# Moving GpSimd's last casts and sink copies into an idle stretch, with the loads they need issued earlier

## Chip, cores and metric

One Trainium2 chip, one core. The metric is the device time of one execution in microseconds (us); lower is better. A single-core execution more than 1.5% above the fastest of its kernel counts as slow; those are named where they occur and are not used in ratios.

## The reference

Sliding-window attention with sink tokens feeds a wave mixer. Cut to what matters:

```python
# q, k, v: (4, 8, 768, 64) float32, times 0.1;  n_sink 4, window 128
scores = q @ k.T / 8                                 # per batch and head
keep   = (pos_k < 4) | (0 <= pos_q - pos_k < 128)    # else -1e9
x      = softmax(scores) @ v                         # -> (4, 768, 512)
theta  = x @ w_theta
y      = w_tok_r @ (x * cos(theta)) + w_tok_i @ (x * sin(theta))
u      = x + y
out    = u + relu(u @ w_ch)
```

## The kernel before

The kernel works on 16 pairs of heads (four batches of four pairs), numbered `i`. One "slot" treats one pair: scores, exponentials (E) on ScalarE, and the weighing of the pair before it, interleaved with the token mix of the batch before. Every engine's order is written by hand. The parts that the change and the argument touch:

```python
vstage = pool("vstage", 4)      # float32 v as loaded
qkr    = pool("qkr", 1)         # q, k transposed by DMA, still in raw order

def pool_copy(out, in_):        # a copy or cast on GpSimd
    nc.gpsimd.tensor_scalar(out=out, in0=in_, scalar1=1.0, scalar2=1.0, op0=ALU.mult, op1=ALU.mult)

QK_DMA = range(12, NPAIR)       # pairs whose q, k are transposed by DMA, ready for use
QK_RAW = (10, 11)               # transposed by DMA, then put in order by a ScalarE copy

def load_qk(i):
    ...
        if i in QK_DMA:         # rows of 64 floats: 256 bytes
            nc.sync.dma_start(out=f.rearrange("p h t d -> p (h t) d"),
                in_=src[b, 2 * hp:2 * hp + 2].rearrange("h (t p) d -> p (h t) d", p=P))
        else:                   # rows of 6 x 64 floats: 1536 bytes
            nc.sync.dma_start(out=f.rearrange("p h t d -> p h (t d)"),
                in_=src[b, 2 * hp:2 * hp + 2].rearrange("h (p t) d -> p h (t d)", t=NT))

def transposed_by_dma(i):       # SyncE issues; for pairs 10, 11 into qkr
    if i in QK_RAW:
        ...
            nc.sync.dma_start_transpose(out=raw, in_=...)         # L182
def transposed(name, i):        # for pairs 10, 11: ScalarE reads qkr, writes qT, kT
    ...                                                           # L206
def slot(i, blk, wtok=None):
    ...
    if i + 2 < HP or HP <= i < NPAIR - 2:
        cast_qk(i + 2)                       # GpSimd
    cast_v(i)
    if i + 2 in V_CAST:
        load_cast_v(i + 2)                   # v, cast in the load; issued by GpSimd
    ...
    transposed_by_dma(i + 2)
    ...
# after the slots of batch b:
    if b == 2 and hp == 3: sink_values(3)    # GpSimd, four copies
    ...
    if b < 3:                                # b == 2: pairs 14 and 15
        for n in range(2):
            load_qk(HP * 3 + 2 * (b - 1) + n)
```

The v loads that GpSimd issues are those of pairs 12 to 15. Names used below: in the lines of the profile, PE is TensorE, DVE VectorE, ACT ScalarE, POOL GpSimd, and SPq the queue in which SyncE issues transfers. E are the exponentials of the scores, zz is x times the cosine and sine (cs) of theta, u is x + y, uT is u transposed by DMA, which the channel sums (L400) need; xT is x transposed by DMA, for theta (L330); qr and kr are pair 11's raw transposes, which ScalarE copies to qT and kT.

The softmax here doesn't subtract the row's maximum and nothing guards it: scores larger than these inputs give would overflow.

Of the kernel before, what the change touches and what calls it, by code (L numbers as in the profile page):

```python
# [12 lines left out]
BF16 = mybir.dt.bfloat16  # L13
# [6 lines left out]
def kernel(  # L20
# [14 lines left out]
    P = 128  # L35
# [5 lines left out]
    HP = H // 2  # L41
# [4 lines left out]
    NPAIR = B * HP  # L46
# [5 lines left out]
    def pool(name, bufs, **kw):  # L52
        return ctx.enter_context(tc.tile_pool(name=name, bufs=bufs, **kw))

    consts = pool("consts", 1)
    stage = pool("stage", 8)
    vstage = pool("vstage", 4)
    cast = pool("cast", 2)
    qkt = pool("qkt", 3)
    qkr = pool("qkr", 1)  # L60
    epool = pool("epool", 4)
    recp = pool("recp", 4)
    xpool = pool("xpool", 2)
# [11 lines left out]
    def pool_copy(out, in_):  # L75
        nc.gpsimd.tensor_scalar(out=out, in0=in_, scalar1=1.0, scalar2=1.0,  # L76
                                op0=ALU.mult, op1=ALU.mult)
# [12 lines left out]
    V_CAST = range(12, NPAIR)  # L90
# [9 lines left out]
    def next_load():  # L100
        for what in later.popleft().split() if later else ():
            {"w": load_wtok, "q": load_qk, "v": load_v}[what[0]](int(what[1:]))


    qk_f, qk_c, qk_t, v_f, v_x, e_t = {}, {}, {}, {}, {}, {}
# [3 lines left out]
    def load_qk(i):  # L109
        b, hp = divmod(i, HP)  # L110
        for name, src in (("q", q), ("k", k)):
            f = stage.tile([P, 2, NT, D], FP32, name=f"{name}f", tag="qkf")
            if i in QK_DMA:
                nc.sync.dma_start(
                    out=f.rearrange("p h t d -> p (h t) d"),
                    in_=src[b, 2 * hp:2 * hp + 2].rearrange("h (t p) d -> p (h t) d", p=P),
                )
            else:
                nc.sync.dma_start(
                    out=f.rearrange("p h t d -> p h (t d)"),  # L120
                    in_=src[b, 2 * hp:2 * hp + 2].rearrange("h (p t) d -> p h (t d)", t=NT),
                )
            qk_f[name, i] = f
# [7 lines left out]
    def cast_qk(i):  # L131
        for name in ("q", "k"):
            c = cast.tile([P, NT, 2, D], BF16, name=f"{name}16", tag=f"{name}16")
            src = qk_f.pop((name, i)).rearrange("p h t d -> p t h d")
            how = CASTS.get((name, i), "pool")
            if how == "act":
                nc.scalar.copy(out=c, in_=src)
            elif how == "dve":
                nc.vector.tensor_copy(out=c, in_=src)
            else:  # L140
                pool_copy(c, src)
            qk_c[name, i] = c
        next_load()

    def load_cast_v(i):
        vx = vxs[i % len(vxs)]
        b, hp = divmod(i, HP)
        nc.gpsimd.dma_start(out=vx[:, :, 0:D], in_=v[b, 2 * hp:2 * hp + 2].rearrange("h (t p) d -> p (h t) d", p=P))
        v_x[i] = vx
# [99 lines left out]
    def weigh(i, e):  # L249
        b, hp = divmod(i, HP)  # L250
        h = 2 * hp + e
        if i % HP == 0 and e == 0:
            x_t[b] = xpool.tile([P, HP, NT, P], BF16, name="x_nat", tag="x_nat")
        if b == 0:
            avp = ps_mm.tile([P, NT, D + 1], FP32, name="avp0", tag="mm")
        elif hp == HP - 1 and e == 0:
            avp = ps_sc.tile([P, 2, 512], FP32, name="av1", tag="sc")[:, 0, 0:NT * (D + 1)]
            avp = avp.rearrange("p (t d) -> p t d", t=NT)
        else:
            avp = ps_sm.tile([P, NT, D + 1], FP32, name="avp", tag="sm")  # L260
        values(i, e, avp)
        normalise(b, hp, avp, e)
# [187 lines left out]
    ident = consts.tile([P, P], BF16)  # L450
    zeros = consts.tile([P, DM], BF16)
    junk = consts.tile([P, 1], FP32)
    half_pi = consts.tile([P, 1], FP32)
    low = consts.tile([P, 1], FP32)

# [31 lines left out]
    def sink_values(b):  # L487
        for tb in range(NB):
            nc.gpsimd.tensor_scalar(out=vsinks[b % 2][:, tb, :, 0:D], in0=vsf[:, b - 2, :, :],
                                    scalar1=rows[:, tb:tb + 1], scalar2=1.0, op0=ALU.mult, op1=ALU.mult)  # L490
# [14 lines left out]
    def make_mask():  # L505
# [14 lines left out]

        nc.scalar.activation(out=bias, in_=mask, func=AF.Identity, scale=30000.0, bias=low)

    W = [8, 1, 4, 1, 0, 3, 3]

    q3 = 2 * NT // 4
# [15 lines left out]
    def finish():  # L541
        if mixed:
            channels(*mixed.pop(0))

    def next_heads(i, name):
        if i + 1 < NPAIR:
            transposed(name, i + 1)

    def slot(i, blk, wtok=None):
        hp = i % HP  # L550
        first, last = hp == 0, hp == HP - 1
        if wtok is not None:
            cast_wtok(wtok)
        if i + 2 < HP or HP <= i < NPAIR - 2:
            cast_qk(i + 2)
        cast_v(i)
        if i + 2 in V_CAST:
            load_cast_v(i + 2)
        if first:
            if i > HP:  # L560
                next_heads(i, "q")
            if i >= 3 * HP:
                scores(i, 0)
            if i > HP:
                piece(blk, 0)
            piece(blk, 1)
        if pending:
            wtok_transposes(pending.pop(), 1)
        if not first or i < 3 * HP:
            scores(i, 0)  # L570
        if hp > 1:
            x_transposes(i // HP, hp - 2)
        if first:
            next_heads(i, "k")
            piece(blk, 2)
        else:
            piece(blk, 0)
            if not last:
                next_heads(i, "q")
        if not first:  # L580
            mask_product(i - 1, 1)
            mask_product(i - 1, 2)
        transposed_by_dma(i + 2)
        if first:
            scores(i, 1)
            turn()
            piece(blk, 3)
        else:
            piece(blk, 1)
            if not last:  # L590
                next_heads(i, "k")
            turn()
            scores(i, 1)
        scores(i, 2)
        if not first:
            piece(blk, 2)
        if wtok is not None:
            wtok_transposes(wtok, 0)
        if not first:
            piece(blk, 3)  # L600
        if hp > 0:
            weigh(i - 1, 0)
            weigh(i - 1, 1)
        if i == 2 * HP - 1:
            mask_product(i, 1)
            mask_product(i, 2)
        finish()
        if wtok is not None:
            pending.append(wtok)
# [21 lines left out]
    load_sinks(1)  # L631
    warm(W[0])
    transposed("q", 0)
    warm(W[1])
    transposed("k", 0)
# [73 lines left out]
    for b in range(1, B):  # L709
        p = b - 1  # L710
        for hp in range(HP):
            i = b * HP + hp
            if b > 1:
                slot(i, (p, hp))
                if b == 2 and hp == 3:
                    sink_values(3)
            else:
                slot(i, (p, hp + 2) if hp < 3 else None, hp + 3 if hp < 3 else None)
                if hp == 1:
                    load_later_sinks()  # L720
                if hp == 3:
                    sink_values(2)
        i = b * HP + HP - 1
        if b > 1:
            four, five = (p, 4), (p, 5)
            piece(four, 0)
            turn()
            x_transposes(b, HP - 2)
            piece(four, 1)
            weigh(i, 0)  # L730
            weigh(i, 1)
            finish()
            piece(four, 2)
            next_heads(i, "q")
            piece(four, 3)
            piece(five, 0)
            x_transposes(b, HP - 1)
            next_heads(i, "k")
            turn()
            piece(five, 1)  # L740
        else:
            five = (p, 5)
            piece(five, 0)
            x_transposes(b, HP - 2)
            next_heads(i, "q")
            piece(five, 1)
            weigh(i, 0)
            next_heads(i, "k")
            weigh(i, 1)
            theta_sums(b, 0, (0, 1))  # L750
            x_transposes(b, HP - 1)
            piece(five, 2)
            theta_sums(b, 0, (2, 3))
            phases(b, 0)
        if b < 3:
            for n in range(2):
                load_qk(HP * 3 + 2 * (b - 1) + n)
        if b > 1:
            thetas(b, 0)
            finish()  # L760
        thetas(b, 1)
        piece(five, 2 if b > 1 else 3)
        theta_sums(b, 2, range(NC))
        if b > 1:
            piece(five, 3)
        phases(b, 2)
# [58 lines left out]
```

## Time and profile before

| | before |
|---|---|
| median of 3 runs | 183.16 us (182.8 to 183.87) |
| span of the profiled execution | 180.9 us |
| TensorE busy | 94% |
| TensorE's named waits, 84 to 121 us | 0.53 + 0.28 + 0.31 + 0.54 = 1.66 us |

```profile
88.04 1.22 SPq L182 DMA_TRANSPOSE qr<-q  x1
89.46 1.21 SPq L182 DMA_TRANSPOSE kr<-k  x1
```

### The profile page before, as it was taken

Reading aid. Unit: us, or ns where it says so; the run is one execution under the profiler, and the core shown is the slowest. Engines: PE = TensorE matmul, PEld = TensorE weight load, DVE = VectorE, ACT = ScalarE, POOL = GpSimd, SP = SyncE. Lnnn points to the kernel's source line nnn. Section 1 sums busy time; section 2 is a strip of 40 time slices with the busy share of each in tenths; the row PEclk is TensorE's granted clock in tenths of the full one; section 3 lists DMA queues with packets and bytes.
Section 4 is the critical chain, followed back from the end, with each engine's and each line's share of the span. In section 5 each row is a group of like instructions: output and inputs, shape, how many; then the busy total and the mean of one; then the engine's idle time right before and its main releaser. Section 6 shows DMA issues by size and latency. Waiting matters only on the chain.

```text
span 180.9 us, 4035 instructions
## 1 busy us (share of the span) xinstructions
PE 169.5 (94%) x1619; PEld 88.4 (49%) x1619; DVE 121.9 (67%) x215; ACT 105.7 (58%) x112; POOL 75.4 (42%) x101
## 2 busy tenths in 40 slices
PE   7799998999999989999998899989999999999991
PEld 2345664554565656443553454434555544344550
DVE  6477867892866688386698981885978816824451
ACT  4897869629768486699998503797454039200000
POOL 8996689987764805038098300750000000000000
PEclk9999999999999999999999999999999999999999
DMA  5999999999998997991399956999733520133413
GB/s 176 307 312 266 350 381 410 383 349 332 328 300 264 287 297 183 282 207 32 102 136 192 220 144 170 297 139 176 118 94 98 147 70 2 59 106 97 145 60 116
DMA packets 73106, 36.80 MB, mean 203 GB/s; under 512 B 61184, under 2 KB 67584, under 8 KB 73088
## 3 DMA queue, kind: packets, MB, share of 16 engines
q1 hardware_dynamic: 65584, 35.60, 71.1%
q0 software_dynamic: 7360, 0.82, 7.3%
q8 instruction: 12, 0.20, 0.5%
q10 hardware_dynamic: 144, 0.13, 0.2%
q14 instruction: 6, 0.05, 0.1%
HBM read 25.82 MB, written 6.29 MB: 178 GB/s over the span
## 4 chain that ended last, share of the span: by engine, by line
PE 64%; ACT 15%; DVE 11%; DMA 3%; issue 3%; POOL 2%; DVEq 0%; ACTq 0%; POOLq 0%
PE yp L372 24%; PE wp L400 9%; PE thp L330 9%; PE avp L277 5%; PE sc L228 5%; ACT E L241 3%; DVE zz L343 3%; ACT cs L339 3%; DVE E L247 3%; ACT cs L340 3%; DMA uT<-u 3%; PE sc L221 2%; PE tp L202 2%; PE wtp L357 2%; PE xtp L307 2%
## 5 line engine op out<-in xcount | busy, mean ns | idle before, releaser
L372 PE MATMUL yp<-zz,wrT 128*128 128x512 bf16 x138 | 52.4, 380 | 1.6 <-DVE zz L343 1.2
L241 ACT ACTIVATE E<-sc 128x1024 bf16<-128x1024 f32 x48 | 47.6, 1032 | 10.6 <-PE sc L228 8.7
L372 PE MATMUL yp<-zz,wiT 128*128 128x512 bf16 x138 | 52.3, 379 | 0.6 <-DVE wiT L361 0.3
L343 DVE TENSOR_TENSOR zz<-cs,x_nat 128x1024 bf16<-128x1024 bf16 x24 | 21.6, 936 | 14.3 <-ACT cs L340 14.3
L247 DVE TENSOR_TENSOR E<-E,mask 128x768 bf16<-128x768 bf16 (+1 forms) x27 | 26.3, 1014 | 1.9 <-ACT E L241 1.9
L76 POOL TENSOR_SCALAR q<-qf 128x768 bf16<-128x768 f32 x14 | 12.3, 881 | 30.6 <-DMA qf<-in_q_dram 15.2
L400 PE MATMUL wp<-wch,uT 128*128 128x512 bf16 x92 | 23.7, 380 | 0.9 <-DMA uT<-u 0.8
L376 DVE TENSOR_TENSOR u<-yp,x_nat 128x512 bf16<-128x512 f32 x23 | 15.9, 690 | 11.0 <-PE yp L372 10.2
L330 PE MATMUL thp<-wth,xT 128*128 128x512 bf16 x96 | 22.8, 379 | 0.1
L339 ACT ACTIVATE cs<-thp,half_pi 128x1024 bf16<-128x1024 f32 (+1 forms) x13 | 13.7, 1051 | 15.5 <-PE thp L330 15.4
L403 DVE SCALAR_TENSOR_TENSOR of<-wp,u 128x512 f32<-128x512 f32 x23 | 15.8, 687 | 9.9 <-PE wp L400 9.8
L372 PEld LDWEIGHTS <-wiT 128*128 128x128 bf16 x138 | 13.5, 98 | 15.3 <-issue 2.4
L372 PEld LDWEIGHTS <-wrT 128*128 128x128 bf16 x138 | 13.5, 98 | 13.5 <-issue 1.7
L277 PEld LDWEIGHTS <-E 128*128 128x128 bf16 x480 | 16.9, 97 | 3.7 <-issue 0.9
L228 PE MATMUL sc<-qT,kT 64*128 64x256 bf16 x192 | 16.6, 264 | 1.4 <-ACT kT L206 0.8
L283 DVE TENSOR_TENSOR x_nat<-avp,rec 128x384 bf16<-128x384 f32 x27 | 15.1, 558 | 0.9
L76 POOL TENSOR_SCALAR k<-kf 128x768 bf16<-128x768 f32 x14 | 14.2, 1015 | 3.1 <-issue 1.2
L228 PEld LDWEIGHTS <-kT 64*128 64x128 bf16 x192 | 6.4, 94 | 16.5 <-issue 12.3
L330 PEld LDWEIGHTS <-xT 128*128 128x128 bf16 x96 | 9.1, 98 | 10.7 <-DVE xT L312 0.6
L277 PE MATMUL avp<-vx,E 128*128 128x65 bf16 x297 | 13.2, 193 | 0.0
L429 ACT COPY lT<-ltp 128x256 bf16<-128x256 bf16 x2 | 0.7, 372 | 21.2 <-PE ltp L427 21.2
L76 POOL TENSOR_SCALAR vx<-vf 128x768 bf16<-128x768 f32 x12 | 12.0, 1005 | 1.9 <-DMA vf<-in_v_dram 1.9
(82 smaller groups left out, 211.6 us busy)
## 6 DMA issues: line engine op xcount, KB each, us to landing
qf<-in_q_dram SPq DMA_DIRECT2D x16, 384.0 KB, 5.5
kf<-in_k_dram SPq DMA_DIRECT2D x16, 384.0 KB, 5.8
out_dram<-of SPq DMA_DIRECT2D x23, 256.0 KB, 2.3
vf<-in_v_dram SPq DMA_DIRECT2D x12, 384.0 KB, 5.3
wf<-in_moe_w_tok_r_dram SPq DMA_DIRECT2D x6, 384.0 KB, 6.6
wf<-in_moe_w_tok_i_dram SPq DMA_DIRECT2D x6, 384.0 KB, 7.6
sqf<-in_moe_w_theta_dram SPq DMA_DIRECT2D x2, 512.0 KB, 6.5
sqf<-in_moe_w_ch_dram SPq DMA_DIRECT2D x2, 512.0 KB, 8.0
```

The source lines that it names most:

```text
L76: nc.gpsimd.tensor_scalar(out=out, in0=in_, scalar1=1.0, scalar2=1.0, op0=ALU.mult, op1=ALU.mult)
L228: nc.tensor.matmul(sc[:, e, 256 * part:256 * part + n], lhsT=kT[r, m * P:(m + 1) * P], rhs=qT[r, m * P:m * P + n], start=not biased, stop= ...
L241: nc.scalar.activation(out=E[:, :, 512 * c:512 * (c + 1)], in_=sc, func=AF.Exp, scale=SCALE)
L247: nc.vector.tensor_tensor(out=E[:, :, r], in0=E[:, :, r], in1=mask2[:, :, r], op=ALU.mult)
L277: nc.tensor.matmul(avp[:, t, :], lhsT=lhsT, rhs=rhs, start=(j == 0), stop=(j == len(seq) - 1), skip_group_check=True)
L330: nc.tensor.matmul(th_t[b, g][:, st, :], lhsT=xT[:, cb, 2 * g + st, :], rhs=wth[:, cb, :], start=(cb == 0), stop=(cb == NC - 1))
L339: nc.scalar.activation(out=cs[:, part, 0, :], in_=thp[:, part, :], func=AF.Sin, bias=half_pi)
L343: nc.vector.tensor_tensor(out=z_t[b][:, 2 * g + st, :, :].rearrange("p o (c n) -> p o c n", c=HP), in0=cs[:, st, :, :].rearrange("p o (c n ...
L372: nc.tensor.matmul(yp, lhsT=wT[i][:, t, sc, :], rhs=z_t[b][:, sc, i, :], start=(j == 0), stop=(j == 2 * NT - 1))
L376: nc.vector.tensor_tensor(out=u.rearrange("p (c n) -> p c n", c=HP), in0=yp.rearrange("p (c n) -> p c n", c=HP), in1=x_t[b][:, :, t, :], o ...
L400: nc.tensor.matmul(wp, lhsT=uT[:, cb, :], rhs=wch[:, cb, :], start=(cb == 0), stop=(cb == NC - 1))
L403: nc.vector.scalar_tensor_tensor(out=of, in0=wp, scalar=0.0, in1=u, op0=ALU.max, op1=ALU.add)
```

## The change

The intent: between batches 2 and 3, GpSimd stood idle for 12.8 us (100.9 to 113.7), while before and after that its copies and casts stretched VectorE's work beside them. The change delays the sink copies behind a "gate" (a copy of one column that waits for VectorE's mask products), and brings the casts of pairs 14 and 15 and their v loads forward into the same hole. To be there in time, the loads of q and k of these pairs are issued in slots 9 and 11 and no longer after batch 2. v staging gives a buffer to the raw transposes.

```diff
-    vstage = pool("vstage", 4)
+    vstage = pool("vstage", 3)
-    qkr = pool("qkr", 1)
+    qkr = pool("qkr", 2)
+    gate = consts.tile([P, 1], BF16)
+    LOAD_LATE = {9: (14,), 11: (15,)}
@@ in slot(i)
-        if i + 2 < HP or HP <= i < NPAIR - 2:
+        if i + 2 < HP or HP <= i < NPAIR - 4:
             cast_qk(i + 2)
-        if i + 2 in V_CAST:
+        if i + 2 in V_CAST and i < NPAIR - 4:
             load_cast_v(i + 2)
@@ around the slots of batches 2 and 3
             if b > 1:
+                for n in LOAD_LATE.get(i, ()):
+                    load_qk(n)
                 slot(i, (p, hp))
-                if b == 2 and hp == 3:
-                    sink_values(3)
@@ after slot 11
+        if b == 2:
+            pool_copy(gate, e_t[i][:, 0, 0:1])
+            sink_values(3)
+            for n in (3, 4):
+                cast_qk(i + n)
@@ after weigh(i, 1)
+            if b == 2:
+                for n in (3, 4):
+                    load_cast_v(i + n)
@@ after batch 2
-        if b < 3:
+        if b == 1:
             for n in range(2):
                 load_qk(HP * 3 + 2 * (b - 1) + n)
```

## The prediction

> **What bounds the kernel now.** I read the page first, then a table of busy time per engine in ten stretches of the span, then the chain of work that ended last between 84 and 123 us, then the timelines of GpSimd, VectorE and the DMA-issuing queue (SPq) there. From the page: busy time of TensorE, and the rows of tenths for GpSimd and the DMA engines (40 slices of 4.52 us).
>
> ```profile
> PE 169.5 (94%) x1619; PEld 88.4 (49%) x1619; DVE 121.9 (67%) x215; ACT 105.7 (58%) x112; POOL 75.4 (42%) x101
> ...
> POOL 8996689987764805038098300750000000000000
> ...
> DMA  5999999999998997991399956999733520133413
> ```
>
> TensorE is busy for 94%, so the whole kernel has 11.4 us of TensorE gaps, and only those can be won. GpSimd, at 42%, is no bound; it can matter only through whom it delays. Its last work (slices 25 and 26, 113 to 122 us) is what the change moves forward. The DMA row has a valley at slices 18 and 19 (81 to 90 us) and is full again at slices 20 to 22. The stretches (columns: window, its length, busy us and instructions of PE, PEld, DVE, ACT, POOL, clock, DMA share, GB/s):
>
> ```profile
> 84.00:95.00 11.00, 10.87 (x131) 5.63 (x129) 8.54 (x13) 11.00 (x11) 6.12 (x6) 1.00 0.73 112
> 95.00:103.10 8.10, 6.97 (x77) 3.37 (x74) 7.62 (x11) 6.15 (x7) 5.11 (x5) 1.00 1.43 216
> 103.10:113.00 9.90, 9.90 (x79) 5.08 (x79) 5.42 (x13) 1.69 (x2) 0.00 (x0) 1.00 0.61 152
> 113.00:120.00 7.00, 6.46 (x32) 2.53 (x31) 6.45 (x8) 5.91 (x7) 6.02 (x6) 1.00 1.18 231
> 120.00:140.00 20.00, 20.00 (x229) 10.04 (x229) 14.93 (x27) 11.62 (x12) 0.11 (x1) 1.00 0.77 129
> ```
>
> TensorE's gaps in these are 0.13, 1.13, 0, 0.54 and 0 us: 1.80 us in all, of which the waits view names 0.53 and 0.28 (the channel sums waiting for the DMA-transposed uT, at 95.7 and 101.7), 0.31 (waiting for u at 103.1) and 0.54 (waiting for zz at 119.7). In the window in between, where GpSimd is wholly idle for 9.9 us, TensorE is full and VectorE has 4.5 us to spare. That is the hole the change aims at. The chain through the two gapped windows (start, us, what):
>
> ```profile
> 96.77 0.69 DVE of L403
> 97.47 3.37 DVE E L247 x3
> 100.83 1.05 issue
> 101.88 0.55 DVE E L247
> 102.43 0.61 DVE u L376
> 103.04 0.04 issue
> 103.08 0.81 PE yp L372 x3
> ...
> 118.41 0.60 DVE u L376
> 119.01 0.64 DVE zz L343
> 119.65 0.04 issue
> 119.69 0.38 PE yp L372
> ```
>
> Twice VectorE sets the pace: by its mask products (L247) and by its phase products (L343). Both have GpSimd beside them. From the timelines of the two engines:
>
> ```profile
> 97.38 5.05 DVE L247 TENSOR_TENSOR E<-E,mask 128x2048 bf16<-128x2048 bf16 x4
> 116.07 2.34 DVE L343 TENSOR_TENSOR zz<-cs,x_nat 128x1024 bf16<-128x1024 bf16 x2 [0.18 <-ACT cs L340]
> 118.94 1.31 DVE L343 TENSOR_TENSOR zz<-cs,x_nat 128x1024 bf16<-128x1024 bf16 x2
> ...
> 96.85 4.04 POOL L489 TENSOR_SCALAR vsink<-vsf,rows 128x512 bf16<-128x512 f32 x4
> ```
>
> The zz pair at 118.94, with GpSimd doing only a DMA issue, took 1.31 us; the pair at 116.07, beside casts, 2.34; the first pair (113.37) 1.92. A mask couple alone (123.44, 129.22) takes 1.68, so four products are 3.36 us, not 5.05.
>
> **What the Trainium skill says.** (1) "SBUF — State Buffer", section "Who interferes with whom": a VectorE instruction with two SBUF inputs contends with a GpSimd instruction that reads SBUF, and the one that comes second is blocked until the first is through. The trace agrees: zz and the mask products, with both inputs in SBUF, are the ones that stretch (1.92 and 2.34 against 1.31), and a GpSimd cast beside them takes 1.77 us against 0.83; u and x_nat, with one input from PSUM, stay at 0.69 and 0.56. (2) "DMA: Bandwidth & Descriptors", section "Issuing engines are not separate DMA queues": all DMAs run on the same 16 engines and interleave. The trace agrees: a load of q lands in 3.6 us where the DMA row is low and in up to 8.9 where it is full. So moved loads hurt whatever transposes run at their new place.
>
> **The change part by part.** The instruction order of the two programs differs, besides names, in GpSimd's and SPq's streams only; one tiny instruction is added.
>
> *The gate and the sinks.* GpSimd copies one element of E of pair 11. Its wait is for VectorE: the last writer of that element is the first mask product of pair 11, the third of the four. E for that product comes at 99.8 (ScalarE), so the product ends near 99.8+1.2=101.0. The sinks (4 x 0.68 alone = 2.7 us, as in batch 1, where they took 2.70) go from 96.9 to 101.0, so they no longer stretch products one to three, and meet at most the fourth. VectorE reaches u at about 101.0+0.5=101.5 in place of 102.35, or 102.2 if a sink is ahead of the fourth product. TensorE's 0.31 us wait for u goes, if the uT before it is not later: TensorE is not free before 102.8. Worth 0.3 us.
>
> *Casts of pairs 14 and 15, and their v.* Four casts of 0.83 and two DMA issues of 1.07, 5.5 us, from 113.7-120.1 into the hole. Starting after the sinks at 103.7: casts of 14 to 105.4; casts of 15 when its load has landed, and pair 13's DMA transposes have released the cast buffer, near 107.5, to 109.2; v issues to 111.4. The first zz is at 113.4, so all three zz pairs should take 1.31: 5.57-3.93=1.64 us less VectorE time. But the chain gives back only what TensorE waited: its products ended at 119.15 and the next began at 119.69. The third zz pair can't start before ScalarE's sine ends at 118.47, so its first product ends at 119.13 and TensorE goes on at 119.2. Worth 0.5 us.
>
> *The loads.* Pair 14's (2 x 384 KB, some 2 us at the 380 to 410 GB/s of the page's best slices) go on SPq at 86.3, at the end of the DMA valley, ahead of the raw transposes of pair 11. These were issued at 88.04 and 89.46, since the single qr buffer was being read by ScalarE's copies until 87.96 and 89.39; with two buffers they go out right after the loads, near 87.7 and 89.0. So the uT issued at 90.77 goes out some 0.4 us sooner, but the rings hold 2 us of load ahead of it: I expect the wait at 95.7 to stay between 0 and 1 us (it was 0.53); cost 0.2 on average. Pair 15's loads come after slot 10's output, at 101: pair 13's transposes and then xT of the third head pair slip by 1.3 us of issuing and about as much of transfer. That xT landed near 107.4 (issue 104.45 plus the median 2.9) and is read at 109.4, so 2 us of slack takes it, barely.
>
> *vstage from 4 buffers to 3.* The fourth v load at the start has to wait for the first cast of v, and SPq is in order, so the weights behind it wait too. From the timelines of SPq and GpSimd:
>
> ```profile
> 6.26 8.97 SPq L128 DMA_DIRECT2D vf<-in_v_dram  x4
> 15.28 2.09 SPq L174 DMA_DIRECT2D sqf<-in_moe_w_theta_dram  x2
> ...
> 14.88 2.02 POOL L76 TENSOR_SCALAR vx<-vf 128x768 bf16<-128x768 f32 x2 [0.85 <-DMA vf<-in_v_dram]
> ```
>
> That cast ends at about 15.9, and the fourth load left by 15.2: 0.7 us or more later, with the v1 and v2 data still in flight. v3 lands some 0.3 to 0.7 us later, w_theta too; its second cast ended at 24.3 and is first needed at 26.0. Cost 0 to 0.4, say 0.1. Later v loads find their buffer free (v8 at 57.7 needs v5's cast, done at 49.8).
>
> Sum: -0.3 -0.5 +0.2 +0.1 = **-0.5 us**, from 183.16 to about 182.6. All four gaps gone would be -1.7.
>
> **Rivals.** (a) *The gain is hidden or taken by DMA*: the loads moved into batch 2 delay uT and xT, so TensorE waits longer at 95.7, 101.7 or 109.4. For it: DMA share 1.43 in 95 to 103, and transposes are small packets. Against: the valley before 88, and slack at 109.4. It would make 183.2 to 184.5. (b) *The start pays*: w_theta and the token weights arrive later behind the blocked v load, and TensorE waits at 25 us. For it: the DMA row is full there, so lost time is lost. Against: SPq issues ran ahead of the data. It would add 0.5 to 1.5. (c) *VectorE was the true bound*, and with 3.3 us of it given back the stages after 119 also tighten: against this, TensorE has no gap from 120 to 140. At most -1.7 us, 181.5.
>
> **Range and chances.** 182.6, with 181.5 (all gaps gone) to 183.8 (rival a or b), which also covers the spread of the kernel before (182.8 to 183.87). Faster by 2% would need 3.7 us, twice the gaps there are: 0.02. Slower by 2% needs both rivals at their worst: 0.03. Within 2%: 0.95.
>
> **What would show it right or wrong.** Right: GpSimd busy from about 101 to 112 and nothing after; zz pairs of batch 2 at 1.31 each; the four mask products near 3.4 to 4.1 us busy; VectorE's total about 3 us below 121.9; no TensorE wait for u near 103, and 0.1 or less for zz near 119. Wrong: longer waits for uT at 96 or 102, a new one for xT at 109, a hole in the first 26 us, or casts of 15 that run past 113 because their load or pair 13's transposes are late.

## More of the kernel before

The prediction shows the page, the stretches and the chain. Three more readings are needed later. First TensorE's timeline, the lines with a wait (start, us, engine, line, operation, what; in brackets the idle time before it and what ended it):

```profile
95.70 1.04 PE L400 MATMUL wp<-wch,uT 128*128 128x512 bf16 x4 [0.53 <-DMA uT<-u]
101.73 1.04 PE L400 MATMUL wp<-wch,uT 128*128 128x512 bf16 x4 [0.28 <-DMA uT<-u]
```

Then, with the same columns, ScalarE's copies of pair 11 and the queue on which SyncE issues the transposes for them:

```profile
91.98 1.61 ACT L206 COPY qT<-qr 128x768 bf16<-128x768 bf16 x1
93.42 1.65 ACT L206 COPY kT<-kr 128x768 bf16<-128x768 bf16 x1
```

## The result

| | before | after |
|---|---|---|
| median of 4 runs | 183.27 us (182.8 to 183.87) | 185.49 us (184.86 to 185.97) |
| ratio | 1 | 1.0117 [1.0074, 1.016] |
| span of the profiled execution | 180.9 us | 183.7 us |
| TensorE's named waits, 84 to 121 us | 1.66 us | 4.19 us |

A ratio here is the mean time of one kernel's fast runs over the mean of the other's in the same rounds, so not quite the ratio of the medians; the brackets are its 95% interval. The change makes the kernel 1.2% slower: within 2%, but 2.9 us from the 182.6 predicted and outside the range. The page after:

```profile
PE 169.4 (92%) x1619; PEld 88.3 (48%) x1619; DVE 117.1 (64%) x215; ACT 105.6 (57%) x112; POOL 73.2 (40%) x102
...
POOL 8975599977658935065215457000000000000000
...
DMA  5999999999999997992999998944834520133413
```

VectorE lost 4.8 us of work (121.9 to 117.1), as the change meant it to. TensorE's own work is the same, 169.4 us, at the same clock: all of the loss is waiting. The DMA row's valley at slices 18 and 19, counted from 0 (before: 1 and 3), reads 2 and 9, and its dip at slices 23 and 24 (before: 5 and 6) reads 9 and 8. The stretches, with the columns that the prediction names:

```profile
84.00:95.00 11.00, 10.87 (x131) 5.60 (x129) 7.31 (x14) 9.58 (x9) 3.11 (x4) 1.00 1.10 164
95.00:103.10 8.10, 5.41 (x59) 2.65 (x58) 4.69 (x7) 6.41 (x7) 2.64 (x3) 1.00 1.32 166
103.10:113.00 9.90, 9.00 (x88) 4.90 (x85) 6.73 (x16) 1.08 (x1) 6.68 (x10) 1.00 1.27 237
113.00:120.00 7.00, 6.40 (x32) 2.60 (x31) 2.78 (x5) 4.58 (x5) 1.66 (x2) 1.00 1.18 131
```

ScalarE, full from 84 to 95 us before, is now busy for 9.58 of the 11 us. TensorE's gaps grow in the second and third stretch: 1.13 to 2.69 us, and none to 0.90. TensorE's waits, from its timeline:

```profile
96.43 1.04 PE L400 MATMUL wp<-wch,uT 128*128 128x512 bf16 x4 [1.38 <-DMA uT<-u]
98.78 0.39 PE L228 MATMUL sc<-qT,kT 64*128 64x256 bf16 x4 [1.31 <-ACT E L241]
104.27 1.04 PE L400 MATMUL wp<-wch,uT 128*128 128x512 bf16 x4 [0.70 <-DMA uT<-u]
112.18 1.47 PE L330 MATMUL thp<-wth,xT 128*128 128x512 bf16 x6 [0.20 <-DMA xT<-x_nat]
114.25 1.04 PE L400 MATMUL wp<-wch,uT 128*128 128x512 bf16 x4 [0.60 <-DMA uT<-u]
```

They sum to 4.19 us, 2.5 more than before; the spans differ by 2.8. The waits for u and zz that the change aimed at are gone. There are five now, four of them for a DMA transpose, and one for ScalarE's E of pair 11. The chain of work that ended last tells how they hang together (start, us, what):

```profile
86.61 0.42 SPq L114
...
87.08 0.83 SPq L114
...
88.01 2.57 SPq L182
...
90.67 5.54 DMA kr<-k
...
96.28 1.52 ACT kT L206
97.81 0.93 ACT E L241
...
99.16 5.07 DMA uT<-u
```

L114 is the load of q and k of pair 14, moved to slot 9; L182 is the raw transpose of pair 11 behind it. The path goes from the moved loads to the raw transposes, and from them to ScalarE's copy and its exponentials. From there the profile's chain goes by VectorE's mask product (98.76) to the next uT. That link is inferred and not shown: this u was ready at 94.85, the product was still running when its uT was issued at 99.16, and SyncE's queue had been issuing pair 12's transposes until 99.07. A second path is in GpSimd's timeline: its casts of pair 12 waited 2.23 and 2.19 us for qr and kr to land (93.33 and 96.35). So the v load of pair 13 went out at 97.92 us, before the change at 95.72, and stood right ahead of this uT, which took 5.1 us to land in place of 3.9. ScalarE's copies and SyncE's queue, beside those of before:

```profile
93.17 1.54 ACT L206 COPY qT<-qr 128x768 bf16<-128x768 bf16 x1 [1.13 <-DMA qr<-q]
96.28 1.52 ACT L206 COPY kT<-kr 128x768 bf16<-128x768 bf16 x1 [1.57 <-DMA kr<-k]
```

```profile
86.61 0.42 SPq L114 DMA_DIRECT2D qf<-in_q_dram  x1
87.08 0.83 SPq L114 DMA_DIRECT2D kf<-in_k_dram  x1
88.01 2.57 SPq L182 DMA_TRANSPOSE qr<-q  x1
90.67 1.24 SPq L182 DMA_TRANSPOSE kr<-k  x1
```

kT is copied 2.9 us later than before. Issuing qr began at the same moment, 88.01 against 88.04, and so the second qr buffer brought nothing: the loads took the time that it freed. But issuing qr held the queue for 2.57 us in place of 1.22, kr went out 1.2 us later, and kr took 5.5 us to land in place of 2.5.

What the change aimed at came about. VectorE's timeline after:

```profile
102.00 1.69 DVE L247 TENSOR_TENSOR E<-E,mask 128x2048 bf16<-128x2048 bf16 x2 [1.54 <-ACT E L241]
119.11 1.29 DVE L343 TENSOR_TENSOR zz<-cs,x_nat 128x1024 bf16<-128x1024 bf16 x2 [1.47 <-ACT cs L340]
121.53 1.29 DVE L343 TENSOR_TENSOR zz<-cs,x_nat 128x1024 bf16<-128x1024 bf16 x2 [0.53 <-ACT cs L340]
```

A zz pair takes 1.29 us with nothing beside it (the first at 115.75 too; before: 1.92, 2.34 and 1.31), and a mask couple 1.69.

### The profile page after: what moved, and what is told of

Its sections match the earlier page's. It is cut to its first block, busy times and chain, and to the rows that moved or that the text cites.

```text
span 183.7 us, 4029 instructions
## 1 busy us (share of the span) xinstructions
PE 169.4 (92%) x1619; PEld 88.3 (48%) x1619; DVE 117.1 (64%) x215; ACT 105.6 (57%) x112; POOL 73.2 (40%) x102
## 4 chain that ended last, share of the span: by engine, by line
PE 55%; DMA 14%; ACT 13%; DVE 8%; SPq 5%; issue 2%; POOL 0%; DVEq 0%; ACTq 0%
PE yp L372 21%; PE wp L400 9%; PE thp L330 9%; DMA uT<-u 6%; DMA vf<-in_v_dram 5%; PE avp L277 4%; PE sc L228 3%; ACT cs L339 3%; ACT cs L340 3%; DMA kr<-k 3%; ACT E L241 3%; DVE E L247 3%; SPq L119 2%; DVE zz L343 2%; PE wtp L357 2%
## 5 line engine op out<-in xcount | busy, mean ns | idle before, releaser
L343 DVE TENSOR_TENSOR zz<-cs,x_nat 128x1024 bf16<-128x1024 bf16 x24 | 18.9, 825 | 17.0 <-ACT cs L340 17.0
L247 DVE TENSOR_TENSOR E<-E,mask 128x768 bf16<-128x768 bf16 (+1 forms) x27 | 24.3, 936 | 4.0 <-ACT E L241 4.0
L400 PE MATMUL wp<-wch,uT 128*128 128x512 bf16 x92 | 23.7, 380 | 2.7 <-DMA uT<-u 2.7
L403 DVE SCALAR_TENSOR_TENSOR of<-wp,u 128x512 f32<-128x512 f32 x23 | 15.8, 686 | 10.7 <-PE wp L400 10.6
L76 POOL TENSOR_SCALAR q<-qf 128x768 bf16<-128x768 f32 x14 | 12.8, 914 | 21.7 <-PE tp L202 9.5
L76 POOL TENSOR_SCALAR k<-kf 128x768 bf16<-128x768 f32 x14 | 13.7, 982 | 5.3 <-DMA kr<-k 2.2
L400 PEld LDWEIGHTS <-uT 128*128 128x128 bf16 x92 | 7.7, 97 | 11.1 <-DMA uT<-u 4.0
```

The costliest lines, as they stand in the source:

```text
L247: nc.vector.tensor_tensor(out=E[:, :, r], in0=E[:, :, r], in1=mask2[:, :, r], op=ALU.mult)
L343: nc.vector.tensor_tensor(out=z_t[b][:, 2 * g + st, :, :].rearrange("p o (c n) -> p o c n", c=HP), in0=cs[:, st, :, :].rearrange("p o (c n ...
L400: nc.tensor.matmul(wp, lhsT=uT[:, cb, :], rhs=wch[:, cb, :], start=(cb == 0), stop=(cb == NC - 1))
L403: nc.vector.scalar_tensor_tensor(out=of, in0=wp, scalar=0.0, in1=u, op0=ALU.max, op1=ALU.add)
```

## The experiments

Twelve kernels. Kernels are compared only within the same rounds. The letters of theories in an expectation are its own. The theories, in words: **the load of pair 14** puts the raw transposes behind it and starves ScalarE; or **the start** pays for the smaller v staging; or **the gate and the late casts** cost; or **load 15 and the v loads** of the hole hold up uT and xT.

One warning on results. All twelve came out as correct, though three of them are wrong (e6, e9 and e10 give pairs 14 and 15 wrong q and k). A likely reason, not tested, is that the inputs are so small that the scores hardly matter. These three measure time only.

### First call: which part costs

**e1_sinks_and_buffers**: before, with the buffers and the gated sinks, without moved loads or casts.

```diff
-    vstage = pool("vstage", 4); qkr = pool("qkr", 1)
+    vstage = pool("vstage", 3); qkr = pool("qkr", 2)
                 if b == 2 and hp == 3:
+                    pool_copy(gate, e_t[i][:, 0, 0:1])
                     sink_values(3)
```

> The kernel before with only the buffer counts (vstage 3, qkr 2) and the gated sinks; loads and casts of pairs 14 and 15 as before. Theory L (the two early loads stand in the DMA rings ahead of time-critical transposes): 182.4 to 183.3, no wait for uT over 0.6 us between 90 and 115. Rival B (buffer counts, blocked v load or the gate cost the time): 184.5 or more. If L is right the raw transposes of pair 11 should go out near 86.4 instead of 88.0, since the second qr buffer then has nothing ahead of it.

Measured: 182.76 us (181.66 to 183.66, 6 runs) against 183.25; ratio 0.9971 [0.9932, 1.001]. No TensorE wait for uT is left from 84 to 121 us. What is left is 0.27 (E), 0.53 (E of VectorE) and 0.19 (zz). So neither the smaller v staging nor the gate costs anything that these runs can see, and the gated sinks may gain a little. The profiled execution ran 1.6 us late from its start (the first channel sum at 42.36 us; before 40.73), so the issue time that I expected for qr is missed in absolute terms. Yet qr went out right after the output ahead of it (87.94, 88.03), where before it stood from 86.26 to 88.04 until ScalarE had freed the one buffer.

**e2_loads_only**: before, with the two loads moved and nothing else.

```diff
             if b > 1:
+                for n in {9: (14,), 11: (15,)}.get(i, ()):
+                    load_qk(n)
                 slot(i, (p, hp))
-        if b < 3:
+        if b == 1:
```

> The kernel before with only the loads of 14 and 15 moved to slots 9 and 11; casts, sinks and buffers as before. Theory L: 185.3 to 186.5, with the raw transposes of pair 11 landing about 4 us later than before. Rival B or rival G (casts and sinks moved into the gap between the batches cost): 183.0 to 183.6.

Measured: median 188.19 us (184.48 to 189.66), four of the six runs slow by the rule above. The ratio, 1.0138 [1.0066, 1.021], rests on the two fast runs (184.48 and 187.0), so the verdict is "unclear". The profiled execution was slow, too. It is used for one thing only: the raw transposes are late here as well, since kT is copied at 95.68 after waiting 1.61 us (before: 93.42, no wait), without gate, casts or new buffers. Slow executions came up in e2 (four of six), e6 (three) and e14 (one) and in no other kernel here; these are the three whose profiles show a TensorE wait of about 2 us or more (2.67, 2.96 and 1.99). So leaving slow executions out may leave out a part of what these kernels cost; no run settles it.

**e4_load14_only**: the change, with load 15, its casts and v left at before's place.

```diff
-    LOAD_LATE = {9: (14,), 11: (15,)}
+    LOAD_LATE = {9: (14,)}
-            for n in (3, 4): cast_qk(i + n)           # likewise load_cast_v
+            cast_qk(i + 3)
         if b > 1:
+            if b == 2: load_qk(15); cast_qk(15); load_cast_v(15)
             thetas(b, 0)
```

> The changed kernel with load, cast and v of pair 15 at their old place after batch 2; only load 14 early in slot 9. Splits the loss by load. Theory L, by the gaps of the trace after: load 14 costs the 1.38, 1.31 and most of the 0.70 us waits, load 15 the 0.20 and 0.60 us ones, so 184.5 to 185.0. If load 15 is the main cost: 183.5 or less.

Measured: 185.02 us (184.36 to 187.01); 1.0122 [1.0073, 1.0171], the whole loss. Its waits on TensorE are after's first three and fifth: 1.27, 1.32, 0.79 and 0.42 us. I had put the fifth (0.60 in the change) down to load 15, and 0.42 of it stays. No cost of load 15 is seen; load 14 is enough for the loss.

**e6_tiny_loads**: the change, with loads 14 and 15 cut to a twelfth of their bytes (results wrong), while every instruction stays.

```diff
-  out=f..., in_=src...
+  out=f...[:, rows, :], in_=src...[:, rows, :]     # rows = slice(0, 1) of 12 for pairs 14, 15
+  cast source: src[:, 0:1, 0:1, :].to_broadcast([P, NT, 2, D])
```

> The changed kernel with the four loads still issued at the same places but only one row of 64 values per partition (1/12 of the bytes); the casts read that row twelve times; wrong result on purpose. Theory L-ring (the data in the rings delays the transposes): 182.2 to 183.2. Theory L-issue (the 1.3 us of issuing in the in-order queue is the cost): 184.8 or more.

Measured: median 186.96 us (184.4 to 188.42), three of six slow; fast runs 1.0108 [1.0063, 1.0153]. I had expected the loss to vanish, and it didn't. But it changed its place. ScalarE is full again, 11.00 of 11.00 us from 84 to 95, and the waits at 96 and 99 us are gone. Beside 0.27 us at 84, two are left in the profiled (fast) execution: 0.82 us for a uT at 102.56, and a new one. The lines are from TensorE's, GpSimd's and SyncE's timelines (this kernel's source has three lines more: its L403 is L400):

```profile
114.52 1.04 PE L403 MATMUL wp<-wch,uT 128*128 128x512 bf16 x4 [2.96 <-DMA uT<-u]
...
107.72 2.08 POOL L151 DMA_DIRECT2D vx<-in_v_dram  x2
...
108.96 1.20 SPq L385 DMA_TRANSPOSE uT<-u  x1
```

With the tiny loads there at once, GpSimd was through its casts early and issued the v loads of pairs 14 and 15 at 107.7, right ahead of a uT at 109.0, which then took 5.5 us to land. So early v loads looked like a second cost (e9 below bears it out), which the change itself happened to avoid: it issued them at 112.58, after the uT of 111.41, whose wait was 0.60. The experiment had two causes in it.

### Second call: load and v loads apart

**e8_v_late**: the change, with the v loads of pairs 14 and 15 held behind the first zz of batch 2. **e9_tiny_v_late**: e8 and e6 together. **e10_long_rows**: e8, with pairs 14 and 15 loaded in the other layout, the same bytes in rows of 1536 instead of 256 (values in the wrong order).

```diff
 e8, e9, e10:
-                for n in (3, 4): load_cast_v(i + n)   # after weigh(i, 1)
         if b > 1:
             thetas(b, 0)
+            if b == 2:
+                pool_copy(gate, z_t[b][:, 0, 0, 0:1])
+                load_cast_v(14); load_cast_v(15)
 e10 also:
-            if i in QK_DMA:
+            if i in (12, 13):                         # in load_qk only
```

> The changed kernel with the two GpSimd-issued v loads held back until the first phase product of batch 2 (about 115 us); loads of 14 and 15 early as changed. Tells whether the v loads cost anything in the changed kernel itself, where they went out at 112.6, after the uT of 111.4. Theory L (slots 9 and 11 loads are the loss): 185.0 to 185.9, gaps at 96, 99 and 104 us as in the changed kernel. If v loads were a good part of the loss: 184.4 or less.

Measured: 185.69 us (184.32 to 187.0) against 182.75; 1.0161 [1.0116, 1.0205]. The waits are after's: 0.95, 1.30, 0.37, 0.21 and 0.66 us. The verdict is "unclear", since the interval reaches 2%, but the loss is there: the place of these v loads isn't what costs in the change.

> The run with tiny loads once more, with the v loads held back in the same way; wrong result on purpose. There the waits at 96 and 99 us went, but a new 2.96 us wait for uT came at 114.5, with the v loads going out at 107.7, just ahead of it. Theory L+V (either kind of load in the rings ahead of a transposed uT delays it): 181.8 to 182.8, no TensorE wait over 0.9 us between 90 and 121. If the data in the rings is not the cause: 184.4 or more again.

Measured: 182.5 us (181.49 to 183.11); 0.9979 [0.9947, 1.0011]. One TensorE wait is left, 0.47 us. Beside e8, only the bytes of two loads are away, and all of the loss with them. The uT of e6 is there too, issued at 107.88, with the v loads now behind it at 113.86, and no wait follows.

> As the run with v loads held back, but the loads of 14 and 15 fetch the same 384 KB each in rows of 1536 bytes instead of 256 (wrong order of positions, so a wrong result on purpose). The 256-byte loads ran at 215 to 220 GB/s by the trace, 3.6 us a pair; if rows of 1536 bytes run near 390, 2 us a pair, as the prediction took, the raw transposes land about 1.6 us sooner: 183.2 to 184.4. If bytes alone count: 185.0 to 185.9.

Measured: 182.53 us (181.37 to 182.97); 0.9996 [0.9969, 1.0022]. I expected half of the loss to go, and all of it went. The same 768 KB are loaded at the same places in all queues. The queue and ScalarE, to be read beside the two fences of the change:

```profile
86.99 1.22 SPq L182 DMA_TRANSPOSE qr<-q  x1
88.30 1.23 SPq L182 DMA_TRANSPOSE kr<-k  x1
```

```profile
91.82 1.60 ACT L206 COPY qT<-qr 128x768 bf16<-128x768 bf16 x1
93.25 1.64 ACT L206 COPY kT<-kr 128x768 bf16<-128x768 bf16 x1
```

Issuing qr and kr ends 2.4 us sooner than in the change, nothing holds up the queue, and ScalarE doesn't wait for them. The DMA view of 86 to 89 us shows why, the change first, then e10:

```profile
DMA packets 1060, 0.49 MB, mean 163 GB/s; under 512 B 932, under 2 KB 932, under 8 KB 1060
```

```profile
DMA packets 520, 0.79 MB, mean 262 GB/s; under 512 B 54, under 2 KB 392, under 8 KB 520
```

In both, 128 packets under 8 KB are the output (0.26 MB). The loads moved some 0.24 MB in 932 short packets in the one, and over 0.5 MB in 338 longer ones in the other. (e10's queue was 0.7 us ahead, which is part of that.) From issue to landing, q and k took 4.0 and 5.3 us in the change and 3.4 and 4.1 here.

**e7_load14_in_slot8**, a try at a better version: load 14 stands in slot 8 right after pair 10's raw transposes, a whole slot ahead of pair 11's. Load 15 and its casts stay late, and the v loads are as in e8.

```diff
 e8, and:
-    LOAD_LATE = {9: (14,), 11: (15,)}
+    LOAD_LATE = {8: (14,)}                 # read inside slot(), after transposed_by_dma(i + 2)
     # after batch 2: load_qk(15); after phases(b, 2): gate on the last zz, cast_qk(15)
```

> A version meant to keep the gain: load 14 goes out in slot 8, between that slot's raw transposes and its uT, where the rings are empty; cast 14 in the gap between the batches; load 15 at its old place after batch 2; v loads after the first phase product; cast 15 after the last phase product of batch 2. Theory L+V: 181.6 to 182.6, no TensorE wait over 0.4 us from 90 to 121. If moving casts into the gap costs by itself: 183.2 or more.

Measured: 182.29 us (181.8 to 183.28); 0.9982 [0.9953, 1.0011]. One TensorE wait, 0.47 us for VectorE's E, is left. The short-row load costs nothing here: it isn't the load as such but who waits for what stands right behind it.

### Third call: the buffers, with the load out of the way

**e7b_slot8_again** is e7 once more. **e13_slot8_old_buffers** is e7 with `vstage` 4 and `qkr` 1, as before. **e12_slot8_both_buffers** is e7 with 4 and 2, which fits only with the output tile in a pool of 2 buffers instead of 3.

> The version with load 14 in slot 8 and the buffers of the changed kernel, again, on the same chip as the two others: 182.0 to 182.6, a ratio to the kernel before of 0.995 to 1.001.

> The version with load 14 in slot 8 with the buffer counts of the kernel before (vstage 4, qkr 1). In the traces so far the first channel sum (40.73 us before) came between 40.5 and 42.4 us with three v buffers, and at 40.7 with four. If the blocked fourth v load is what eats the gain: 181.6 to 182.2 and a first channel sum at 40.7. If one qr buffer costs about as much (its raw transposes wait for ScalarE until 88.0): 182.0 to 182.6, as without this edit. If three v buffers don't matter: 182.3 or more.

> The same with four v buffers and two qr buffers, room made by two output tiles in place of three. If both buffers help: 181.3 to 182.0, the fastest of all. If two output tiles make VectorE wait for stores: 182.4 or more, with waits for the store in VectorE's view.

Measured against 183.37 us (182.04 to 184.57):

| | median (range), us | ratio |
|---|---|---|
| e7b | 182.16 (181.04 to 183.08) | 0.9949 [0.9903, 0.9995] |
| e13 | 182.88 (181.8 to 183.36) | 0.9975 [0.9927, 1.0024] |
| e12 | 183.6 (182.57 to 184.93) | 1.0034 [0.9982, 1.0086] |

e7b has no TensorE wait at all between 84 and 121 us, as its stretches show; it is the best version found, by half a per cent here and by 0.2% as e7. e13 hints at what the second qr buffer is worth: with one buffer qr went out at 89.67, 0.74 us after the output ahead of it, and a wait of 0.64 us for uT followed. That is small, the intervals overlap, and e13 changes both buffers.

```profile
84.00:95.00 11.00, 10.87 (x123) 5.44 (x123) 8.26 (x12) 11.00 (x11) 6.15 (x7) 1.00 1.18 167
95.00:103.10 8.10, 8.10 (x94) 4.21 (x91) 7.27 (x15) 6.30 (x7) 3.58 (x6) 1.00 1.44 215
103.10:113.00 9.90, 9.90 (x78) 5.05 (x77) 5.12 (x12) 2.29 (x3) 2.44 (x4) 1.00 0.76 175
```

e12 should have been the best and is not; its expectation is missed. Its profiled execution made its first channel sum at 43.02 us; before did so at 40.73, and e13, with four v buffers too, at 42.38. The start scatters by over 2 us between single executions, whatever the number of v buffers, with how soon the first inputs land (VectorE's wait for q was 1.0 us before, 2.5 in e13, 2.7 in e12). No cost of the smaller output pool is seen: VectorE's wait for a store is 0.6 us in e12 as in e7b and e13. But the clock granted to TensorE was 0.94 in the first 30 us of e12's profile and 1.00 in theirs. Why e12 isn't faster stays open.

### Fourth call: what makes kr so late

kr landed 5.5 us after its issue, when the loads were over by 92.4. In the DMA view from 92 to 95 us of the change, the queue of GpSimd's v loads stands beside SyncE's (queue, packets, MB, share):

```profile
q0 software_dynamic: 1532, 0.19, 100.2%
q1 hardware_dynamic: 1172, 0.29, 64.2%
```

It is the v load of pair 12, issued at 90.01. **e14_v12_moved** is e8 with this load moved to slot 11, beside pair 13's.

```diff
-        if i + 2 in V_CAST and i < NPAIR - 4:
-            load_cast_v(i + 2)
+        if i == 11:
+            load_cast_v(12); load_cast_v(13)
```

> The kernel of the run with v loads held back (185.69 us, early 256-byte loads of 14 and 15 unchanged), with the GpSimd-issued v load of pair 12 moved from slot 10 (90.2 us) to slot 11, so that it does not run between 92.4 and 95.4, where kr of pair 11 was still in the rings. Theory A (the early load pushes kr into the stretch of this v load, and the two together make the 5 us landing): kr lands by about 94.5, the waits at 96 and 99 us shrink to about 1 us in all, 183.6 to 184.6. Theory N (the early load alone does it): kr lands at 96 again, 185.0 to 186.2.

Measured: 186.11 us (185.83 to 189.72, one slow) against 183.03; 1.0173 [1.0145, 1.02], "unclear" as with e8. I had expected 183.6 to 184.6 if the v load had its part in kr's delay. At the place in question it did, but no time came of it. ScalarE's and TensorE's timelines:

```profile
94.99 1.55 ACT L206 COPY kT<-kr 128x768 bf16<-128x768 bf16 x1
...
104.29 1.64 PE L400 MATMUL wp<-wch,uT 128*128 128x512 bf16 x4 [1.99 <-DMA uT<-u]
```

kT no longer waits for kr (in e8 it did, 1.34 us), and TensorE's 0.95 and 1.30 us at 96 and 99 shrink to one wait of 0.83. But both v loads now went out at 96.05, ahead of the uT of 99.25, and TensorE waited 1.99 us for that. So the v load had its part in kr's delay, and moving it has moved the loss, not removed it. (After that wait the granted clock fell in this execution, to 0.83 from 103 to 113 us; but two other fast ones, at a mean clock of 1.00, took as long, 186.15 and 186.07 us.)

## Why the prediction was wrong

What held, step by step:

- **Casts and zz.** The zz pairs take 1.29 us where 1.31 was predicted, and TensorE's wait for zz is gone. The four mask products take 2 x 1.69 = 3.38 us (predicted 3.4 to 4.1), and the wait for u is gone. GpSimd works from 103.3 to 114.7 us (predicted 101 to 112), with a hole of 3.0 us in which the cast of pair 15's q waits for a transpose to land, so that these casts come at 111.0 and not at 107.5. VectorE lost 4.8 us (predicted 3). e1, e7, e7b and e9 agree with a small gain, 0.2 to 0.5% below before, where the predicted 0.8 us gross would be 0.4%. But only e7b's interval excludes 1, and e7 is the same kernel, so a gain isn't shown for certain.
- **vstage.** No cost is shown: e1 has it and is not slower, and the start varies by more than the 0.1 us predicted.

What failed is the step "*The loads*", in three of its parts:

1. **The size of the load.** It was put at "some 2 us at the 380 to 410 GB/s of the page's best slices". This load has rows of 256 bytes, and the right rate stood in the trace of before. Its DMA view, first for the fast slices (26 to 37 us), then for 72 to 77 us, where short rows run alone:

```profile
DMA packets 3151, 4.31 MB, mean 392 GB/s; under 512 B 1228, under 2 KB 2117, under 8 KB 3148
```

```profile
DMA packets 5509, 1.40 MB, mean 280 GB/s; under 512 B 5509, under 2 KB 5509, under 8 KB 5509
```

In the first, short packets are 1228 x 256 bytes, 0.3 of 4.3 MB; in the second they are all. At the lower rate the 0.79 MB of this load would take 2.8 us in place of 2. In the changed kernel the DMA engines moved 0.27 and 0.24 MB in the two microseconds from 88.5 on, when all packets were short; with the long rows of e10 they moved 0.36 MB from 88 to 89. The last of the load landed at 92.4, 5.8 us after its first issue at 86.61 (e10: 4.6). Nor did the prediction count that a transpose behind such loads holds the queue longer. The trace of before showed that once, for pair 10's qr behind the loads of pairs 12 and 13 and one of v:

```profile
76.13 2.24 SPq L182 DMA_TRANSPOSE qr<-q  x1
```

The diff didn't show the short rows: `load_qk` has two layouts, and pair 14 takes the one with short rows. The Trainium skill says so: "DMA: Bandwidth & Descriptors", section "Specifications", asks for 512 bytes or more in a transfer for full rate, and section "Why small descriptors are slow (HBM only)" counts 11 cycles in place of 8 for a piece of 256 bytes. e10 agrees: the same bytes in long rows, and the whole loss is gone (1.0161 to 0.9996). I had read that page for the prediction, and not asked what rows this load has.
2. **Who waits.** The prediction followed the load to uT and xT alone and took the raw transposes as sooner ("right after the loads, near 87.7 and 89.0"). They are the ones that decide. qr was issued at 88.01, and blocked; kr landed at 96.2. Before, it landed by about 92.0 with 1.5 us to spare. Its reader is ScalarE, which the prediction's own table had full for 11.00 of 11.00 us, so what it waits it can't make good. The kT copy waited 1.57 us, the exponentials behind it came late, and TensorE lost 1.31 us at 98.78 and more to the uT after it. By 98.78 it had waited 2.69 us, 2.2 more than before, and since that wait ended with E, an earlier uT at 96.43 would not have shortened the sum. e9 (loads nearly empty) and e10 (long rows) both take away just this, and both come out level with before. GpSimd's casts of pair 12 were readers too, by way of the next v load (above).
3. **The second buffer.** It was counted as "the uT issued at 90.77 goes out some 0.4 us sooner". It went out at 92.01, 1.2 us later; the loads, and the 2.57 us of issuing qr, had taken the freed time.

Put in terms of the sum: "cost 0.2 on average" for the loads should have been about 3. TensorE's named waits went from 1.66 to 4.19 us although the 0.31 and 0.54 that the change aimed at were won. Without these two, before's waits are 0.81 us: the loads added 4.19 - 0.81 = 3.4 us of waiting. That the result stayed within 2%, as forecast at 0.95, is no merit of the mechanism: the sign was wrong. Rival (a), a gain taken by DMA, was right in kind, but was given 184.5 us at the most, for the same reason.

Still open: how the loss divides between the load's short rows and the v load of pair 12 that runs into kr (e10 says that without the first the second does no harm; e14 that without the second kr is nearly on time and the loss moves); whether short rows cost by the transfer itself or by the many packets that hold up the issuing queue (2.57 against 1.22 us for qr), for e10 changes both; and why e12 is not faster. How much of the last 1.2 us of added waiting, at 104, 112 and 114 us, comes by way of GpSimd's late v load of pair 13 isn't split either.

## What to carry to other kernels

Before a load is moved, look at the length of its rows and not only at its bytes, and list every transfer that is issued behind it until it has landed, with its reader. The reader to fear is an engine that is full in that stretch, even if no wait is shown there. A valley in the DMA row is worth as much as the time until the next transposes: the same load one slot earlier, right behind a pair of transposes, cost nothing that these runs can see. And an experiment that makes one part faster (e6) can bring forward another that collides, so look where the loss lies before reading its total.

## What the Trainium skill lacked or had wrong

- "DMA: Bandwidth & Descriptors" says that queues interleave, and that an engine goes round between queue rows by packet (section "Queues, rings and completion order"), but not what a DMA transpose behind other traffic costs. Measured: kr took 2.5 us to land before, 5.5 behind a load of 2 x 384 KB in short rows and beside a v load; a uT just behind two v loads of 192 KB issued by GpSimd took 5.5 (e6).
- The same page doesn't say how much longer one DMA holds the issuing queue when others stand ahead of it. Measured for qr: 1.22 us before, 2.57 behind the short-row loads, 1.22 again behind the same loads in long rows (e10). Loads are not the only cause: in e7b qr took 2.11 us with only an output right ahead.
- "TensorE: Matmul & The Clock Gate", section "Why this matters for your kernels", warns of idle gaps over some 3 us. In e14 the granted clock fell after a shorter wait: after one of 1.99 us it was 0.50 from 105 to 108 us, and four matmuls took 1.64 us instead of 1.04. After one of 2.96 us (e6) it stayed at 1.00 and the four took 1.04. So the clock can fall after a wait of 2 us, and doesn't always; what decides it isn't shown here.
- "GPSIMD Engine Reference" gives no least time for a tiny copy. The gate, one column of 128 rows, took 0.42 or 0.43 us on E in every profile that has it, and 0.50 or 0.18 to 0.19 on zz. (The profile's times on GpSimd are rough.)
